# One band-attention and MLP kernel on one core: wider early loads, w_out in column halves, four-bank transpose sessions, and the mask copies moved from slot 1 to slot 10

## The chip, the cores and the metric

The kernel runs on one core of one Trainium2 chip. The metric is device time in microseconds (us) of one execution. A core has these engines: TensorE (PE, with its weight loads shown apart as PEld), VectorE (DVE), ScalarE (ACT), GpSimd (POOL) and SyncE (SP), beside 16 DMA engines that move data. SBUF is the memory on the core that the loads fill, PSUM the one that the matmuls write into, in banks. The granted clock is the share of TensorE's full clock that the profile reports for a stretch of time: 1.00 is full, 0.50 half. The time before the change is 321.6 us (median of three runs, 321.3 to 322.24).

## The reference

The reference takes q, k and v for 8 batches, 8 heads, 576 positions and 64 dimensions. It computes attention within a band of 32 positions to each side, and then a two-layer perceptron with a piecewise activation.

```python
scores = scale * np.matmul(q, k.transpose(0, 1, 3, 2))
mask = np.abs(pos[:, None] - pos[None, :]) <= 32
attn = softmax(np.where(mask, scores, -1e9))          # written out in the reference
x = np.matmul(attn, v).transpose(0, 2, 1, 3).reshape(4608, 512)
h = x @ w_in                                          # 512 -> 2048
g = np.where(h >= 1, h, np.where(h <= -1, 0.0, (h + 1) ** 2 / 4))
out = g @ w_out                                       # 2048 -> 512
```

All inputs and the output are float32. The kernel computes in bfloat16.

## The kernel before

The program is a row of numbered slots. Slot a makes one piece of the hidden layer `hp` (256 tokens by 256 columns, 8 matmuls). ACT and DVE turn it into `gT` (ACT: `rr`; DVE: `mx`, then `gT`). What else has to be done is put between the slots by a table: scores, sums (the attention output `xT`), transposes of q and k (`tp`), and quarters of the second matmul (`op`). Each engine takes its instructions in the order of the program.

First come the parts that the change touches in loading. Every load of q and k for batches 0 to 2 is a piece of 32 partitions (72 KB in SBUF, or 144 KB for the first four, which stay float32), and all but the first four are issued by POOL:

```python
def load_long(b, half, t, y, eng=None, x=None):
    src, dst, nm = ((q, qn, "qn"), (k, kn, "kn"))[t]
    ...
    (eng or nc.gpsimd).dma_start(out=dst[b, half][32 * y:32 * y + 32],
                                 in_=src[b].rearrange("(h y) s d -> y h (s d)", h=2)[y]
                                 .rearrange("h (l p j) -> l p h j", l=2, p=32)[half])

def load_w_out(n):                       # 4 of the 16 row blocks, all 512 columns
    nc.gpsimd.dma_start(out=w_out[:, 4 * n:4 * n + 4], in_=...)

for y in range(NY):                      # NY = 4
    load_long(0, 0, 0, y, nc.sync, q32)
for y in range(NY):
    load_long(0, 0, 1, y)
...
w = [(load_w_in, c, c + 256, h) for c in range(0, DFF, 256) for h in range(2)]
put(w[:4] + halves(0, 1) + w[4:])        # halves: eight loads of 72 KB
mix(halves(1, 0), [(load_w_out, 0)])
put([(load_w_out, 1), (load_w_out, 2)] + [(load_v, 1, n) for n in range(4)])
mix(halves(1, 1), [(load_w_out, 3)])
...
```

Then come the parts of the slots. A transpose session of q or k has two parts (5 and 4 blocks of columns, each for two groups of heads, 18 matmuls together). Each part takes a PSUM buffer of pool `ps_s` or `ps_n`, and each pool has one buffer:

```python
quarters = [(9, 0), (11, 4), (12, 1), (13, 5), (13, 2), (14, 6), (15, 3), (15, 7)]
at(1, *through(0, 1, 0), (keep_warm, 4, ps_o, "op"))    # q of batch 0, second half
at(1.5, *through(0, 1, 1))                              # k of batch 0, second half
at(2, (scores, 0, (0, 1), (0, 2), (2, 4)), (scores8, 0, ps_o))
...
    # in the loop over slots a
    if a == 1:
        for h in range(2):                              # four copies on DVE
            for m, n, w in ((mask4, 8, 128), (mask8, 4, TAIL)):
                V.tensor_copy(m[HD[h]]..., band[HD[h], ...].to_broadcast([64, n, w]))
    run(a)
    for x in post:
        quarter(x)
    run(a + 0.5)
```

The softmax here doesn't subtract the row's maximum and nothing guards it: scores larger than these inputs give would overflow.

## Time and profile before

| | before |
|---|---|
| time, median | 321.6 us |
| profiled execution, span | 319.4 us |
| PE busy | 306.2 us, 96% |
| lines of the profile: hp, op, tp, mx, xT | L463, L414, L178, L469, L296 and L299 |

The prediction shows the page, the stretches and the timeline near 20 us. The view below is the list of waits of PE; the columns are the instruction that waited with its line, what it waited for, then us in total, number of times and the longest.

```profile
PE tp L178 <- DVE qT L181: 2.8, 1, 2.8
PE hp L463 <- DVE xT L299: 1.3, 1, 1.3
...
PE tp L180 <- DVE qb L324: 1.1, 1, 1.1
...
PE hp L463 <- DVE xT L296: 0.8, 2, 0.5
PE bb L284 <- DVE xT L296: 0.6, 1, 0.6
```

It is read from the top. The largest single wait of the bound engine is the second k transpose in slot 1, which waits for the DVE copy of qT. Every other wait is smaller, and none of them is for a DMA.

### The profile page before, as it was taken

How to read it: one execution, taken by the hardware profiler on the slowest of the kernel's cores; microseconds unless marked ns; L12 is line 12 of the kernel's file. 1: busy time of each engine (PE TensorE's matmuls, PEld its weight loads, DVE VectorE, ACT ScalarE, POOL GpSimd, SP SyncE). 2: the span in 40 equal slices, each digit the busy share in tenths (PEclk: the TensorE clock that was granted, in tenths of full speed). 3: DMA queues.
4: the chain of work that ended last, by engine and by line, in shares of the span. 5: the costliest groups of instructions: out<-in, count | busy, mean ns of one | idle time of the engine just before them, and what ended most of it. 6: DMA issues, size and time to landing. Idle time of an engine off the chain costs nothing.

```text
span 319.4 us, 8557 instructions
## 1 busy us (share of the span) xinstructions
PE 306.2 (96%) x3651; PEld 201.8 (63%) x3651; DVE 248.9 (78%) x390; ACT 192.9 (60%) x318; POOL 88.6 (28%) x121
## 2 busy tenths in 40 slices
PE   7969899999999999999999999999999999999995
PEld 3547565666666666666666666666666666666652
DVE  3366956787888888888888888888888888878760
ACT  3739656675785576756766666666676766554421
POOL 8786938896204504130501200000000000000000
PEclk9989999999999999999999999999999999999999
DMA  9999999999999999949990956005410000000111
GB/s 146 161 134 182 168 176 166 170 162 164 152 146 160 168 125 186 161 58 110 187 154 36 109 106 110 35 35 108 95 50 35 33 35 35 36 33 35 49 49 66
DMA packets 122661, 34.52 MB, mean 108 GB/s; under 512 B 108800, under 2 KB 117760, under 8 KB 122624
## 3 DMA queue, kind: packets, MB, share of 16 engines
q0 software_dynamic: 93760, 18.06, 74.4%
q1 hardware_dynamic: 28864, 15.93, 21.9%
q8 instruction: 28, 0.46, 0.6%
q14 instruction: 9, 0.07, 0.1%
HBM read 36.70 MB, written 9.44 MB: 144 GB/s over the span
## 4 chain that ended last, share of the span: by engine, by line
PE 85%; DVE 6%; ACT 5%; DMA 1%; issue 1%; SPq 0%; ACTq 0%; DVEq 0%
PE op L414 38%; PE hp L463 37%; PE bb L284 5%; PE bb L218 2%; DVE mx L469 2%; PE tp L178 2%; ACT pt L226 1%; DVE gT L470 1%; DMA q<-in_q_dram 1%; ACT rc L291 1%; ACT lr L290 1%; ACT rr L467 1%; DVE xT L296 1%; PE bb L197 0%; DVE mask L475 0%
## 5 line engine op out<-in xcount | busy, mean ns | idle before, releaser
L463 PE MATMUL hp<-xT,w_in 128*128 128x256 bf16 x1152 | 150.2, 274 | 2.1 <-DVE xT L299 1.3
L414 PE MATMUL op<-w_out,gT 128*128 128x512 bf16 x576 | 146.6, 380 | 0.0
L467 ACT ACTIVATE rr<-hp 128x512 f32<-128x512 f32 x144 | 85.5, 595 | 92.3 <-PE hp L463 91.1
L463 PEld LDWEIGHTS <-w_in 128*128 128x128 bf16 x1152 | 111.7, 98 | 43.9 <-issue 3.1
L469 DVE TENSOR_TENSOR mx<-hp,rr 128x512 f32<-128x512 f32 x144 | 99.2, 689 | 38.7 <-ACT rr L467 36.8
L470 DVE SCALAR_TENSOR_TENSOR gT<-rr,mx 128x512 bf16<-128x512 f32 x144 | 99.6, 692 | 4.9
L414 PEld LDWEIGHTS <-gT 128*128 128x128 bf16 x576 | 53.4, 98 | 41.6
L226 ACT ACTIVATE pt<-bb 128x1024 bf16<-128x1024 f32 (+1 forms) x33 | 33.2, 1011 | 6.5 <-PE bb L218 5.3
L100 POOL DMA_DIRECT2D vn<-in_v_dram x32 | 27.5, 883 | 28.8 <-PE bb L218 28.2
L296 DVE TENSOR_TENSOR xT<-bb,rc 128x512 bf16<-128x512 f32 (+1 forms) x32 | 21.0, 657 | 10.8 <-ACT rc L291 10.2
L419 ACT COPY osb<-op 128x512 f32<-128x512 f32 x36 | 20.8, 581 | 11.6 <-PE op L414 11.2
L291 ACT ACTIVATE rc<-lr 128x512 f32<-128x512 f32 (+2 forms) x40 | 23.5, 587 | 1.3
L92 POOL DMA_DIRECT2D qn<-in_q_dram x10 | 12.3, 1245 | 41.1 <-DMA qT<-qn 41.1
L290 ACT ACTIVATE lr<-bb 128x512 f32<-128x512 f32 (+2 forms) x40 | 22.0, 551 | 0.7 <-PE bb L284 0.6
L284 PE MATMUL bb<-pt,ones 64*64 64x256 bf16 (+3 forms) x352 | 19.5, 255 | 1.3 <-DVE xT L296 0.6
L192 DVE TENSOR_TENSOR pt<-pt,mask 128x1024 bf16<-128x1024 bf16 (+1 forms) x33 | 20.2, 613 | 0.2 <-ACT pt L226 0.2
L284 PE MATMUL bb<-pt,vn 64*64 64x128 bf16 (+3 forms) x712 | 18.2, 204 | 0.0
L284 PEld LDWEIGHTS <-vn 64*64 64x64 bf16 x712 | 16.7, 107 | 0.0
L284 PEld LDWEIGHTS <-ones 64*64 64x64 bf16 x352 | 10.3, 106 | 9.8 <-issue 9.0
L84 POOL DMA_DIRECT2D kn<-in_k_dram x24 | 13.0, 549 | 9.0 <-DMA w_out<-in_moe_w_out_dram 4.1
L218 PE MATMUL bb<-qT,kT 64*64 64x128 bf16 x520 | 13.0, 217 | 0.8 <-DVE kT L181 0.8
L92 POOL DMA_DIRECT2D kn<-in_k_dram x10 | 12.2, 1226 | 3.6 <-DMA kn<-in_k_dram 2.2
(44 smaller groups left out, 102.7 us busy)
## 6 DMA issues: line engine op xcount, KB each, us to landing
out_dram<-osb SPq DMA_DIRECT2D x36, 256.0 KB, 2.4
vn<-in_v_dram POOLq DMA_DIRECT2D x32, 144.0 KB, 6.0
qn<-in_q_dram POOLq DMA_DIRECT2D x10, 288.0 KB, 6.9
kn<-in_k_dram POOLq DMA_DIRECT2D x10, 288.0 KB, 8.9
w_in<-in_moe_w_in_dram POOLq DMA_DIRECT2D x16, 128.0 KB, 5.5
w_out<-in_moe_w_out_dram POOLq DMA_DIRECT2D x4, 512.0 KB, 7.9
kn<-in_k_dram POOLq DMA_DIRECT2D x24, 72.0 KB, 4.0
qn<-in_q_dram POOLq DMA_DIRECT2D x20, 72.0 KB, 5.5
```

What stands on the lines that cost most here:

```text
L92: nc.gpsimd.dma_start(out=x[:, :, h], in_=src[b, NY * h:NY * h + NY].rearrange("y s d -> (y s) d") .rearrange("(u p) d -> p u d", p=128))
L100: nc.gpsimd.dma_start(out=vn[b][64 * a:64 * a + 64, :, h], in_=v[b, y:y + 2].rearrange("y s d -> (y s) d") .rearrange("(c r) d -> r c d", ...
L226: A.activation(p, ps[:, :, :128 * n].rearrange(like, y=m), AF.Exp, scale=D ** -0.5)
L284: nc.tensor.matmul(bb[HD[h], a, o + c0:o + c1], ones[HD[a]] if c is None else vn[b][HD[a], c, h], p(a, h), start=n == 0, stop=True, skip_g ...
L290: A.activation(lr[:, :, :D0], bb[:, :, D0:2 * D0], AF.Ln)
L291: A.activation(rc[:, :, :D0], lr[:, :, :D0], AF.Exp, scale=-1.0)
L296: muls.append(lambda: V.tensor_mul(o, bb[:, :, :D0], rc[:, :, :D0]))
L414: nc.tensor.matmul(o, gT[tt // 2][:, j, 128 * (tt % 2):128 * (tt % 2) + 128], w_out[:, j], start=not done, stop=len(done) == 2 * NF - 1, s ...
L463: nc.tensor.matmul(hp[:, j], w_in[:, kk, 256 * f + 128 * j:256 * f + 128 * j + 128], xT[:, kk, r0:r0 + TB], start=n == 0, stop=n == 3)
L467: A.activation(rr, hp, AF.Relu, scale=0.5, bias=0.5)
L469: V.tensor_max(mx, hp, rr)
L470: V.scalar_tensor_tensor(gT[t][:, 2 * f:2 * f + 2], rr, 1.0, mx, op0=ALU.min, op1=ALU.mult)
```

## The change

The intent is to start the middle of the program sooner and keep PE from standing near 20 us, in four moves:

- q and k of batches 1 and 2 come in one load each, with rows of nine positions per partition. The first half of batch 0 comes in two loads per tensor, q from SP and ACT, k from POOL; so does its second half, all from POOL (four loads where there were eight). The later columns of w_in come in 512-column pieces.
- w_out is loaded in two halves of 256 columns. A pair of token tiles (256 tokens) uses one half at a time, so that the first output matmuls need half of w_out.
- All 36 transposes of one tensor of a batch (in slot 1, those of the second halves of q and k) run as one session over four PSUM banks. The copies to SBUF come after all of them. Four warming matmuls between them go away.
- The four mask copies on DVE go from slot 1 to slot 10.

The places of later scores, sums and transposes in the table move along with these, as the cuts show.

```diff
-    for y in range(NY):
-        load_long(0, 0, 0, y, nc.sync, q32)
-    for y in range(NY):
-        load_long(0, 0, 1, y)
+    for h in range(2):
+        load_half(0, 0, h, (nc.sync, nc.scalar)[h], q32)
+    for h in range(2):
+        load_half(0, 1, h)
 ...
-    w = [(load_w_in, c, c + 256, h) for c in range(0, DFF, 256) for h in range(2)]
-    put(w[:4] + halves(0, 1) + w[4:])
-    mix(halves(1, 0), [(load_w_out, 0)])
-    put([(load_w_out, 1), (load_w_out, 2)] + [(load_v, 1, n) for n in range(4)])
-    mix(halves(1, 1), [(load_w_out, 3)])
+    w = [(load_w_in, c, c + 256, h) for c in range(0, 1024, 256) for h in range(2)]
+    w += [(load_w_in, c, c + 512, h) for c in range(1024, DFF, 512) for h in range(2)]
+    put(w[:4] + [(load_half, 1, t, h) for t in range(2) for h in range(2)] + w[4:])
+    put([(load_w_out, 0, n) for n in range(2)] + [(load_rows, 1, t) for t in range(2)])
+    put([(load_v, 1, n) for n in range(4)] + [(load_w_out, 1, n) for n in range(2)])
 ...
+    def tposes(b, *sets):
+        todo = []
+        for (t, half), pool in zip(sets, (ps_s, ps_n)):
+            tp = pool.tile([128, 2, 8, 128], BF, name="tp", tag="bb")
+            todo += [tpose(b, 2 * half + part, t, (A.copy, V.tensor_copy)[part], tp[:, part]) for part in range(2)]
+        for copy in todo:
+            copy()
 ...
-    quarters = [(9, 0), (11, 4), (12, 1), (13, 5), (13, 2), (14, 6), (15, 3), (15, 7)]
+    pairs = [(10, 0), (10, 1), (11, 2), (12, 3), (13, 4), (14, 5), (15, 6), (16, 7)]
 ...
-    at(1, *through(0, 1, 0), (keep_warm, 4, ps_o, "op"))
-    at(1.5, *through(0, 1, 1))
+    at(1, (tposes, 0, (0, 1), (1, 1)))
 ...
-    for n, a in enumerate((20, 22, 23, 27)):
+    for n, a in enumerate((18, 20, 22, 27)):
         at(a, seq[2 + n][0])
-    for n, a in enumerate((11.5, 12.5, 19, 20, 22, 26, 27)):
+    for n, a in enumerate((13.5, 14.5, 16, 18, 20, 25, 27)):
         at(a, seq[n][1])
 ...
-    for b, half, *a in ((1, 0, 9.5, 10.5), (1, 1, 17.5, 18.5), (2, 0, 24.5, 25.5), (2, 1, 28.5, 29.5)):
+    for b, *a in ((1, 11.5, 12.5), (2, 19.5, 21.5)):
 ...
-        if a == 1:
+        if a == 10:
             for h in range(2):      # the mask copies
```

Left out are the bodies of `load_half`, `load_rows` and `pair`, and the copy orders that belong to the new layouts.

## The prediction

> **What bounds the kernel now.** I read the page first, then the stretches of 2 us, then the timelines of TensorE (PE), VectorE (DVE) and GpSimd (POOL) where a stretch was not full. The kernel is a row of slots: slot n makes one 256-token, 256-column piece of the hidden layer (hp, 8 matmuls), and quarters of the second matmul (op, 4 matmuls), attention pieces and transposes (tp) are put between. From the page:
>
> ```profile
> PE 306.2 (96%) x3651; PEld 201.8 (63%) x3651; DVE 248.9 (78%) x390; ACT 192.9 (60%) x318; POOL 88.6 (28%) x121
> PE   7969899999999999999999999999999999999995
> DMA  9999999999999999949990956005410000000111
> ```
>
> PE is the bound: 306.2 of 319.4 us busy, and in the stretches after 90 us it has no gap until the last tiles. Only the first 90 us and the way the work is filled in there can give anything: 13.2 us of idle in all, some of it (start, end) untouched. The 16 transfer engines are full for the first 60 us or so, so loads may pace what PE gains. In the 2 us stretches (columns: length, busy time of PE, PEld, DVE, ACT, POOL, granted clock, DMA share, GB/s):
>
> ```profile
> 18.00:20.00 2.00, 1.08 (x14) 0.46 (x12) 1.97 (x5) 1.11 (x2) 2.00 (x4) 1.00 1.19 135
> 20.00:22.00 2.00, 0.15 (x4) 0.15 (x5) 1.75 (x4) 0.00 (x0) 2.00 (x4) 0.84 1.21 143
> 22.00:24.00 2.00, 2.00 (x16) 1.28 (x13) 0.72 (x1) 0.00 (x0) 1.18 (x3) 0.50 1.30 160
> ```
>
> PE stands at 20 to 22 us and then runs at half clock: "busy" at 22 us is not full speed. The timeline says why (start, duration, instruction, idle before it and who ended it); PE and DVE rows together:
>
> ```profile
> 18.61 0.47 PE L178 MATMUL tp<-ident,kn 128*64 128x128 bf16 x10
> 19.54 1.51 DVE L475 COPY mask<-band 64x1024 bf16<-64x1024 bf16 x4
> 21.08 0.72 DVE L181 COPY qT<-tp 128x512 bf16<-128x512 bf16 x1
> 21.85 0.64 PE L178 MATMUL tp<-ident,kn 128*64 128x128 bf16 x8 [2.77 <-DVE qT L181]
> 22.42 1.89 PE L463 MATMUL hp<-xT,w_in 128*128 128x256 bf16 x8
> 24.24 0.64 PE L197 MATMUL bb<-bias,ident 64*64 64x512 bf16 x4
> 33.44 1.91 PE L463 MATMUL hp<-xT,w_in 128*128 128x256 bf16 x16 [1.31 <-DVE xT L299]
> 35.19 1.03 PE L414 MATMUL op<-w_out,gT 128*128 128x512 bf16 x4
> 36.77 1.05 PE L463 MATMUL hp<-xT,w_in 128*128 128x256 bf16 x8
> ```
>
> The second k transpose waits for a PSUM buffer that the DVE copy of qT empties; that copy stands behind the mask copies (1.51 us). Loads at this time:
>
> ```profile
> 14.97 1.05 POOL L84 DMA_DIRECT2D kn<-in_k_dram  x2 [1.31 <-DMA w_in<-in_moe_w_in_dram]
> 16.02 6.21 POOL L104 DMA_DIRECT2D w_in<-in_moe_w_in_dram  x10
> ```
>
> POOL waits for an older load before it issues the next. The program order of its instructions shows it: each load waits on one of eight semaphores in turn, so eight loads are in flight at most, and with 72 KB loads that is little (102 GB/s at 16 to 18 us, against 160 to 200 in most stretches).
>
> **What the Trainium skill says.** (1) "TensorE: Matmul & The Clock Gate", What's actually happening: the clock falls to half after an idle window of about 3.4 us and comes back after a busy one. The trace agrees in kind: clock 0.50 after a 2.77 us wait, the 8 hp matmuls spaced over 1.82 us instead of 0.87. (2) "DMA: Bandwidth & Descriptors", Rules for kernel authors: small transfers should be merged into large ones, and two transfers to disjoint partition groups into one of 128 partitions. The trace shows 0.53 us of POOL for each 72 KB load and the slump above. (3) The same page, Issuing engines are not separate DMA queues: issuing from two engines saves only the issuing time. Here one q issue takes about 0.42 us, and q and k together already move 229 and 196 GB/s at 2 to 6 us, so I expect little from the split over SP and ACT.
>
> **The change, part by part** (shifts of PE's position against before; minus is earlier).
>
> 1. *First loads.* q: two issues on two engines in place of four on one (1.80 us of issuing); k: two on POOL in place of four (2.27 us). The 0.59 MB of q and 0.30 MB of k were all moved by 6 us at over 190 GB/s, so the data, not the issue, sets most of it. The q cast at 6.26 us comes perhaps 0.3 us earlier. **-0.3.**
>
> 2. *Slot 1: one session in four banks, masks gone, four warm matmuls gone.* All 36 transposes now run without a wait (2 x 0.63 us after 17.01). The DVE chain is next: its four hp steps end at 19.54, then qT 0.72 and kT 0.72 give 20.98. In the new program the DVE copy of a session also waits for the ACT copy of it, but ACT is done by about 19.2. So the scores of slot 2 start near 21.0 in place of 24.24. hp of slot 2 (0.87) fits in between if its weights are there: they landed at 20.2, and should land one to two us earlier, because their issue no longer waits behind eight q and k loads. **-3.2**, with the 0.85 us of warm matmuls, the 2.77 us wait and the 0.95 us of half clock all within it. About 1.8 us of idle stays (18.9 to 20.7).
>
> 3. *Slots 2 to 8.* ACT is nearly continuous from exp at 25.16 to 32.5, and DVE from 24.98 to 40; both chains are unchanged, so slot 8 (33.44, waiting for xT on DVE) just moves. Weights for slots 4 and 5 landed at 24.5 and 26.2 and would be needed near 23.5; slot 4 now has to wait for a 512-column piece. I reckon on 0 to 1 us there, partly hidden in ACT's queue. **0.**
>
> 4. *Slots 9 and 10.* Before, a quarter of op (0.87) and 18 transposes (0.63) filled PE at 35.19 to 36.77 while DVE caught up: mx and gT take 0.68 + 0.69 us a slot against 0.87 for hp. Now five hp groups stand in a row, and the fifth needs a PSUM buffer that mx of slot 8 frees (ends 36.64 before). PE stands 1.5 us there; the same work comes later. **+1.5.**
>
> 5. *w_out in column halves.* 64 matmuls of 512 columns become 128 of 256. The last 36 op matmuls take 7.78 us (0.216 each), eight hp matmuls of 256 columns 0.87 (0.109 each), with weight loads of 98 ns beside them: 13.9 us either way. **0.** It lets the first pairs run with half of w_out (1.05 MB) and q and k come sooner.
>
> 6. *Slots 10 to 16.* The masks (1.51) and more DVE copies of transposes fall here, where DVE had 0.9 to 1.2 us idle a slot; I find no wait longer than 0.3 on PE from it. One score set gets its mask from DVE (0.68) in place of PE (-0.25). Up to slot 16 there are 36 more transposes (+1.26) and one quarter less (-0.87). Before slot 16 the chain sums, Ln, exp, xT took 2.8 us (49.4 to 52.19) with two quarters (1.73) under it and 0.52 idle; now only one pair (0.87) lies under it: idle 1.3. **+0.14 + 0.8.**
>
> 7. *Slots 17 to 30.* The second session of each tensor of batch 1 is gone, the work above is paid back (-0.39). Before, PE gaps add up to about 3.8 us between 52 and 88 us (0.57 three times and 0.31, 0.80, 0.25 at attention pieces, and 0.09 at each edge of a transpose). Now two gaps of about 0.9 (sums of slots 20 and 22 waiting for the last DVE copy, itself behind ACT's) and small ones, 2.4 in all. **-0.4 - 1.4.**
>
> After slot 30 nothing changes. Sum: -0.3 - 3.2 + 1.5 + 0.14 + 0.8 - 0.39 - 1.4 = **-2.85 us**, 321.6 to about **318.8 us**.
>
> **Rivals.** (a) *Loads take over*: w_in of slots 4 to 7, or q and k of batch 1, which are now needed whole at slots 11 and 12. At 0.168 MB/us and 4.99 MB moved at 32 us, the 6.4 MB up to k are there near 40.5 us; PE would want them near 40.7. For it: DMA is full. Against it: fewer, larger loads fill the slump. It would leave a gain of 1 us or none (320.5 to 321.5). (b) *All stalls of the first 90 us vanish, nothing replaces them*: 2.8 + 1.3 + 0.8 + 0.6 + 0.5 + 0.4 of waits, 0.85 warm, 1.2 clock: some 8 us, 313. Against it: five hp in a row outrun DVE, and one pair under the slot 15 chain. (c) *The clock falls again*: the 1.8 us left idle near 20 us may still bring half clock; about +1 us (319.8). (d) *DVE becomes the bound* in slots 10 to 16 by masks and copies: another +1.
>
> **Range and chances.** (a), (c), (d) push up by 1 each, (b) in part pulls down by 2: 316.3 to 321.0. Faster by 2% needs under 315.2, which only most of (b) gives: 0.06. Slower by 2% needs a new bound of 6 us: 0.01.
>
> **What would show it.** Right: no PE wait for qT near 20 us, clock 1.0 at 22 us, slot 8 near 30 us; then an hp wait of about 1.5 us for DVE at slot 10, one of over 1 us for xT at slot 16, two of 0.9 at slots 20 and 22; PE busy for op and hp unchanged. Wrong: PE or its weight loads waiting for w_in, qn, kn or w_out; a clock below 1 after 20 us; a start of hp before 14 us or after 15.

## The result and the profile after

| | before | after |
|---|---|---|
| time, median of four runs | 321.46 us (321.3 to 322.24) | 317.26 us (316.82 to 317.79) |
| ratio, with 95% interval | 1 | 0.987 (0.9851 to 0.9888) |
| span of the profiled execution | 319.4 us | 315.0 us |

A ratio here, and below, is the mean time of one kernel's runs over the mean of the other's runs of the same rounds, so it is not quite the ratio of the medians that stand beside it. The kernel is 1.3% faster, which is inside the 2% band called "same". The gain is 4.2 us where 2.85 was predicted.

From the page of the changed kernel (busy us, share of the span and number of instructions; then tenths in 40 slices):

```profile
PE 298.4 (95%) x3670; PEld 207.7 (66%) x3707; DVE 250.8 (80%) x393; ACT 192.1 (61%) x316; POOL 69.5 (22%) x83
PE   8987998999999999999999999999999999999995
DMA  9999999999999969997993983005501100100111
```

The PE row has the same form: full from the eighth slice to the last but one, with all other holes before. The busy time of PE must not be compared with the 306.2 of before: 477 records of `op` from L424 are in this trace where the program has 512, and the holes of the missing ones show as 4.8 us of waits for "issue". The position of an instruction is a safer measure, and I use it from here on. DVE is 1.9 us busier, and POOL went from 121 to 83 instructions.

The 2 us stretches answer to those in the prediction (length, busy time of PE, PEld, DVE, ACT and POOL, granted clock, DMA share, GB/s):

```profile
18.00:20.00 2.00, 1.44 (x12) 0.92 (x12) 1.97 (x5) 1.06 (x2) 2.00 (x3) 1.00 1.27 202
20.00:22.00 2.00, 1.86 (x52) 1.42 (x55) 1.35 (x3) 1.39 (x4) 1.98 (x3) 1.00 1.25 208
22.00:24.00 2.00, 2.00 (x81) 1.66 (x70) 1.36 (x2) 1.97 (x5) 0.85 (x1) 1.00 1.26 194
```

From 20 to 22 us PE is busy for 1.86 us rather than 0.15. From 22 to 24 us the granted clock is 1.00 rather than 0.50, and 81 matmuls, many of them small ones of attention, fit where 16 did. The data rate is about 200 GB/s where it was 135 to 160.

The timeline of PE (start, duration, instruction, idle before it and who ended it):

```profile
16.77 0.90 PE L183 MATMUL tp<-ident,kh 128*64 128x128 bf16 x18
18.19 1.03 PE L484 MATMUL hp<-xT,w_in 128*128 128x256 bf16 x8 [0.52 <-DVE mx L490]
19.53 0.41 PE L202 MATMUL bb<-bias,ident 64*64 64x512 bf16 x4 [0.31 <-DVE qT L186]
20.14 0.42 PE L223 MATMUL bb<-qT,kT 64*64 64x128 bf16 x16 [0.20 <-DVE kT L186]
...
28.90 1.91 PE L484 MATMUL hp<-xT,w_in 128*128 128x256 bf16 x16 [1.05 <-DVE xT L304]
...
32.15 1.03 PE L484 MATMUL hp<-xT,w_in 128*128 128x256 bf16 x8 [1.34 <-DVE mx L490]
33.02 1.91 PE L440 MATMUL op<-w_out,gT 128*128 128x256 bf16 x16
```

And of DVE:

```profile
18.16 0.69 DVE L491 SCALAR_TENSOR_TENSOR gT<-rr,mx 128x512 bf16<-128x512 f32 x1
18.77 0.71 DVE L186 COPY qT<-tp 128x512 bf16<-128x512 bf16 x1
19.38 0.71 DVE L186 COPY kT<-tp 128x512 bf16<-128x512 bf16 x1
...
35.40 1.19 DVE L496 COPY mask<-band 64x1024 bf16<-64x1024 bf16 x4
```

The transposes of k now run without the 2.77 us wait. The hidden piece of slot 2 follows at 18.19 (22.42 before), and slot 8 begins at 28.90 (33.44 before). Slot 10 waits 1.34 us for `mx`, which is the new wait that the prediction had named. The waits of PE, in the same columns as before:

```profile
PE hp L484 <- DVE mx L490: 1.9, 2, 1.3
...
PE hp L484 <- DVE xT L301: 1.1, 3, 0.5
PE hp L484 <- DVE xT L304: 1.1, 1, 1.1
PE bb L289 <- DVE kT L186: 0.8, 1, 0.8
PE bb L289 <- DVE qT L186: 0.8, 1, 0.8
PE bb L289 <- DVE pt L197: 0.4, 1, 0.4
```

With the smaller ones that are not shown, and without those for the first warm-up data and for issue, the listed waits add up to 6.6 us, against 7.8 before. So the waits alone do not make the 4 us: the warming matmuls and the half clock, which count as busy, are in it too, and many of the waits have only changed place. None is for a DMA. The two of 0.8 are the sums of slots 20 and 22, which wait for the last DVE copy of a transpose session.

The issues of POOL (start, duration of the group, instruction, idle before and who ended it):

```profile
11.46 1.93 POOL L109 DMA_DIRECT2D w_in<-in_moe_w_in_dram  x3 [0.16 <-issue]
14.62 2.45 POOL L109 DMA_DIRECT2D w_in<-in_moe_w_in_dram  x4 [1.23 <-DMA w_in<-in_moe_w_in_dram]
```

The weights of slot 2 are issued at 11.5 and 12.1 us and land at 17.4 and 18.1. Before, they were issued at 16.0 and 16.6 us and landed at 19.5 and 20.2.

Where the time went can be read from the starts of the same work in both traces:

| work | before, us | after, us | shift | step's own part |
|---|---|---|---|---|
| slot 0, hp | 14.79 | 14.01 | -0.78 | -0.78 |
| slot 2, scores | 24.67 | 20.14 | -4.53 | -3.75 |
| slot 8, hp | 33.44 | 28.90 | -4.54 | -0.01 |
| slot 16, second part of hp | 52.25 | 50.00 | -2.25 | +2.29 |
| slot 31, hp | 89.64 | 85.65 | -3.99 | -1.74 |
| last hp | 306.65 | 302.67 | -3.98 | +0.01 |
| end of span | 319.4 | 315.0 | -4.4 | -0.4 |

The column at the right is the difference of two neighbouring shifts. Everything is decided by 86 us; between slot 31 and the last hp nothing changes. The last 0.4 us is not work that the change touched: the last output transfer lands at 318.1 us before and at 314.1 after, a shift of -4.0, so the rest lies in the end of the program behind that.

Part of the gain is the clock, and the runs of the kernel before show how much. Of its 33 timed runs in the three sets of experiments, the 24 with a granted clock of 0.995 or lower have a median of 321.66 us, the 9 with 0.997 or higher one of 320.4 us. So about 1.3 us is at stake in whether the clock falls, and the other 3 us of the gain do not need that fall.

### The profile page after: what moved, and what is told of

Same layout as the page of the kernel before. It is cut to its first block, busy times and chain, and to the rows that moved or that the text cites. A ratio compares the mean times of both kernels' runs of the same rounds, so it can differ in the third digit from the quotient of the medians.

```text
span 315.0 us, 8563 instructions
## 1 busy us (share of the span) xinstructions
PE 298.4 (95%) x3670; PEld 207.7 (66%) x3707; DVE 250.8 (80%) x393; ACT 192.1 (61%) x316; POOL 69.5 (22%) x83
## 4 chain that ended last, share of the span: by engine, by line
PE 86%; DVE 5%; ACT 5%; issue 3%; ACTq 0%
PE hp L484 37%; PE op L424 35%; PE bb L289 5%; PE op L440 4%; PE bb L223 2%; PE z L332 2%; DVE mx L490 2%; ACT pt L231 1%; ACT rc L296 1%; DVE gT L491 1%; PE tp L183 1%; DVE xT L301 1%; ACT lr L295 1%; DVE kT L186 1%; DVE qT L186 1%
## 5 line engine op out<-in xcount | busy, mean ns | idle before, releaser
L424 PE MATMUL op<-w_out,gT 128*128 128x512 bf16 x477 | 123.0, 379 | 5.0 <-issue 4.8
L424 PEld LDWEIGHTS <-gT 128*128 128x128 bf16 x512 | 47.6, 98 | 36.7
L301 DVE TENSOR_TENSOR xT<-bb,rc 128x512 bf16<-128x512 f32 (+1 forms) x32 | 21.1, 658 | 11.1 <-ACT rc L296 10.4
L429 ACT COPY osb<-op 128x512 f32<-128x512 f32 x32 | 18.7, 583 | 11.5 <-PE op L424 11.1
L197 DVE TENSOR_TENSOR pt<-pt,mask 128x1024 bf16<-128x1024 bf16 (+1 forms) x34 | 21.0, 616 | 0.2 <-ACT pt L231 0.2
L440 PE MATMUL op<-w_out,gT 128*128 128x256 bf16 x128 | 16.3, 273 | 0.0
L97 POOL DMA_DIRECT2D kn<-in_k_dram x10 | 12.1, 1213 | 9.7 <-PE tp L183 3.9
L440 PEld LDWEIGHTS <-gT 128*128 128x128 bf16 x128 | 12.1, 98 | 1.7
## 6 DMA issues: line engine op xcount, KB each, us to landing
qn<-in_q_dram POOLq DMA_DIRECT2D x2, 576.0 KB, 14.7
```

What stands on the lines that cost most here:

```text
L97: nc.gpsimd.dma_start(out=x[:, :, h], in_=src[b, NY * h:NY * h + NY].rearrange("y s d -> (y s) d") .rearrange("(u p) d -> p u d", p=128))
L424: nc.tensor.matmul(o, gT[tt // 2][:, j, 128 * (tt % 2):128 * (tt % 2) + 128], w_out[:, j], start=not done, stop=len(done) == 2 * NF - 1, s ...
L440: nc.tensor.matmul(o[:, tt], gT[p][:, j, 128 * tt:128 * tt + 128], w_out[:, j, 256 * half:256 * half + 256], start=not done, stop=len(done ...
```

## The experiments

The theory to be tested: about 3.8 us are gained in slot 1, by (i) the mask copies moving away from the qT and kT copies, so that PE neither waits nor loses its clock, together with (ii) merged loads that bring the weights of slots 2 and 3 in time. About 2.3 us are given back in slots 9 to 16, by work placed so that PE waits for DVE. About 1.7 us come back in slots 17 to 30 through fewer copies and waits.

The rivals: the loads alone do it, and the masks do not matter; or the warming matmuls that went are what was gained; or the +2.3 us is contention on DVE and not a matter of placing. Each run was timed in five rounds against the kernel before on the same chip; the medians of the kernel before in the three sets are 321.55, 321.63 and 321.38 us.

| run | median us | ratio to before (95%) |
|---|---|---|
| masks back in slot 1 | 319.61 | 0.9938 (0.9915 to 0.9962) |
| warm matmuls back | 317.43 | 0.9875 (0.9855 to 0.9896) |
| before, masks in slot 10 | 320.0 | 0.9962 (0.9943 to 0.9982) |
| first loads in parts | 318.43 | 0.9915 (0.9893 to 0.9936) |
| second half of batch 0 in parts | 320.26 | 0.9969 (0.994 to 0.9998) |
| pair 0 in slot 9 | 316.83 | 0.9849 (0.9825 to 0.9872) |
| pair 7 in slot 15 | 316.06 | 0.9835 (0.9812 to 0.9858) |
| batch 2's sessions moved | 316.1 | 0.9833 (0.9811 to 0.9855) |
| after, unedited | 317.1 | 0.9875 (0.9843 to 0.9908) |
| w_out in row pieces | 317.99 | 0.99 (0.9873 to 0.9926) |
| three moves together | 315.48 | 0.9815 (0.9791 to 0.9839) |
| the same, one sums piece later | 314.6 | 0.9791 (0.9764 to 0.9818) |

### Masks back in slot 1

```diff
--- after
-        if a == 10:
+        if a == 1:
```

> The changed kernel with the mask copies put back from slot 10 to slot 1, nothing else. Theory (the masks hold up the DVE copies of qT and kT, on which the scores of slot 2 wait): the four copies take 1.2 to 1.5 us, so the scores of slot 2 and all slots up to 8 come 1.2 to 1.5 us later; if PE then idles near 3 us in a row the granted clock falls in the stretch after it and another 0.5 to 1 us is lost. Time 1.2 to 2.2 us over the changed kernel, 318.4 to 319.4. Rival (the four-bank session alone removed the wait, the place of the masks does not matter): no change, 317.0 to 317.5.

The kernel took 319.61 us: about 2.1 us of the change's gain is lost (0.9938 less 0.987 to 0.9875 of some 321 us). That is within the 1.2 to 2.2 us expected, though the median lies 0.2 us above the times named. The PE timeline of this run:

```profile
21.22 0.41 PE L202 MATMUL bb<-bias,ident 64*64 64x512 bf16 x4 [2.10 <-DVE qT L186]
...
22.55 1.89 PE L484 MATMUL hp<-xT,w_in 128*128 128x256 bf16 x8
```

And its stretch from 22 us:

```profile
22.00:24.00 2.00, 2.00 (x35) 1.46 (x28) 1.18 (x2) 1.47 (x3) 0.85 (x1) 0.51 1.27 195
```

With the masks back, the wait for qT is back as 2.10 us even though the transposes are in one session, and the clock is back at half. The eight hp matmuls of slot 3 show 1.89 us, where they show 1.05 at full clock. So the session by itself does not remove the wait; it only moves it from the transposes to the scores. Slot 8 begins at 31.91, 3.0 us later than after. This is one execution with half clock; of the six timed runs one had a clock of 1.000 and still took 319.32 us, so most of the loss needs no fall of the clock. The loads, at 195 GB/s, are as after and cannot be the cause.

### The kernel before with only the masks moved

```diff
--- before
-        if a == 1:
+        if a == 10:
```

> The kernel before with one edit: masks at slot 10 in place of slot 1. Theory: the DVE copy of qT starts at 19.5 in place of 21.1 us, the second k transposes at 20.3, PE's wait falls from 2.8 to about 1.3 us and the clock stays at 1.0 at 22 us; slot 8 starts 2 to 3 us earlier, the time falls by 2 to 3 us to 318.5 to 319.5. Most of the gain of slot 2 is then the masks' alone, and the session adds the last 1 us. Rival (the two-bank session is what holds PE, masks or not): a gain of at most 1.2 us, clock still falling at 22 us.

It took 320.0 us, so 1.2 us (by the ratio) to 1.6 us (by the medians) were gained where 2 to 3 had been expected: a miss. PE's timeline shows both halves of the reason:

```profile
20.33 0.41 PE L178 MATMUL tp<-ident,kn 128*64 128x128 bf16 x8 [1.23 <-DVE qT L181]
...
48.80 1.89 PE L414 MATMUL op<-w_out,gT 128*128 128x512 bf16 x8 [1.99 <-DMA w_out<-in_moe_w_out_dram]
```

The first line is as the theory wants: the wait shrinks from 2.77 to 1.23 us (it remains, I take it, because the sessions here are two-bank ones; that was not run alone), the clock is 1.00 from 20 to 26 us, and slot 8 begins at 30.62, 2.82 us earlier than in the kernel before. The second line is where the gain went: with the loads of the kernel before, PE reaches the output matmuls before the w_out piece is there and waits 1.99 us for it. By the second part of slot 16 (50.74 us) only 1.51 us of the 2.82 are left. Hence rival (a) of the prediction, "loads take over", is real for this kernel. The changed kernel, with its new load order and w_out in halves, shows no such wait.

### The second half of batch 0 in eight loads instead of four

```diff
--- after
+    def load_parts(half, t, eng=None, x=None):      # four loads of 32 partitions, 72 KB each
+        ...
-    put(w[:4] + [(load_half, 1, t, h) for t in range(2) for h in range(2)] + w[4:])
+    put(w[:4] + [(load_parts, 1, t) for t in range(2)] + w[4:])
```

(The copy order of this half changes with its layout.)

> The changed kernel with the second half of batch 0's q and k loaded in eight 72 KB parts again, in place of four loads of 128 partitions. Theory (eight loads in flight at most, so small loads hold up the issue of w_in behind them): w_in of slot 2 is issued near 14 to 15 us in place of 11.5 and lands near 19.5, that of slot 3 near 21.5 to 22.5 in place of 18.7 to 19.4; hp of slot 2 or 3 then waits and slot 8 comes 0.5 to 2 us later, time 317.8 to 319.3. Rival (loads are never on the path here): same landing order with slack, slot 8 at 28.9, time within 0.3 us of the changed kernel.

It took 320.26 us in the median, 319.37 to 322.41, so about 3 us of the gain is lost: the largest effect of any single part taken back, and more than the 0.6 to 2.0 us expected. The profile fell on its slowest execution (322.41), so what it shows is larger than typical. Its waits, from the PE timeline:

```profile
17.93 0.69 PE L191 MATMUL tp<-ident,kh 128*64 128x128 bf16 x18 [0.70 <-DMA kh<-in_k_dram]
20.38 1.03 PE L492 MATMUL hp<-xT,w_in 128*128 128x256 bf16 x8 [1.76 <-DVE kT L194]
...
27.01 1.87 PE L492 MATMUL hp<-xT,w_in 128*128 128x256 bf16 x8 [2.92 <-DMA w_in<-in_moe_w_in_dram]
```

And from POOL's timeline:

```profile
15.34 0.54 POOL L92 DMA_DIRECT2D kh<-in_k_dram  x1 [1.58 <-DMA w_in<-in_moe_w_in_dram]
15.86 4.91 POOL L117 DMA_DIRECT2D w_in<-in_moe_w_in_dram  x8
```

Four more loads, of the same bytes in all, move the first w_in issue after them from 11.46 to 15.86 us, partly because POOL stands 1.58 us until an older load has landed. Slot 2 stands 1.76 us, for the copy of kT by the profile. The w_in piece of slot 4 then comes 2.92 us too late, and in this execution the clock fell during this wait: it was 0.55 from 26 to 28 us, and the eight matmuls at 27.01 show 1.87 us. Two of the six timed runs had a clock of 1.000 and took 319.37 and 319.83 us, so at least 2 us of the loss are there without the fall. The data rate was 90 GB/s from 16 to 18 us, where the changed kernel has 193. Here the masks are in slot 10 and the session is in four banks as after. So moving the masks does not pay in this kernel unless the loads come in time. The two are not all or nothing, however. With all of the change but the masks, slot 8 comes 1.53 us earlier than before; with the masks alone, 2.82 us. Together these are 4.35, near the 4.54 of the changed kernel (one profile each).

### First loads in parts, as before

```diff
--- after
-    for h in range(2):
-        load_half(0, 0, h, (nc.sync, nc.scalar)[h], q32)
-    for h in range(2):
-        load_half(0, 1, h)
+    load_parts(0, 0, nc.sync, q32)
+    load_parts(0, 1)
```

> The changed kernel with the first q and k loads as before: four q loads on SP, four k loads on GpSimd. Theory (the fewer, wider first loads brought the first hp 0.78 us forward): the first hp at 14.7 to 14.8 in place of 14.0 us, the time 0.6 to 0.9 us more, 317.9 to 318.2. Rival (my prediction: the data and not the issue sets it): 0.3 us or less. If the start moves and the end does not, later loads or DVE absorb it.

It took 318.43 us, about 1.2 us more than after, where 0.6 to 0.9 was expected. The start itself moved little: the first hp came at 14.31 us (14.01 after, 14.7 to 14.8 expected). But the w_in of slot 2 is issued at 12.99 rather than 11.46 us, and PE waits for data that it does not wait for after. From its list of waits:

```profile
PE hp L490 <- DMA w_in<-in_moe_w_in_dram: 1.2, 2, 0.7
...
PE tp L189 <- DMA kh<-in_k_dram: 0.6, 1, 0.6
```

Slot 4 begins at 23.88, 1.27 us later than after, of which 0.30 was there at the first hp; slot 8 begins at 30.33, 1.43 us later. (Between them lies a wait of 0.93 us just before slot 5 that the profile puts down to "issue". It is 0.20 us in the first profile of the changed kernel and 1.20 in the repeat below, so I do not count it as an effect of this edit.) The first loads are therefore worth more downstream, through POOL's place in its queue, than at the start.

Why the start moves so little shows when the ACT cast of q and PE's first rows are put side by side. Before:

```profile
6.26 0.62 ACT L325 CAST qb<-q 128x512 bf16<-128x512 f32 x1 [4.24 <-DMA q<-in_q_dram]
6.94 0.68 PE L180 MATMUL tp<-ident,qb 128*128 128x128 bf16 x9 [1.05 <-DVE qb L324]
```

After:

```profile
1.19 5.15 PE L332 MATMUL z<-warm 128*128 128x512 bf16 x14 [1.19 <-DVE warm L126]
4.98 0.62 ACT L339 CAST qb<-q 128x512 bf16<-128x512 f32 x1 [2.29 <-DMA q<-in_q_dram]
6.18 0.67 PE L185 MATMUL tp<-ident,qb 128*128 128x128 bf16 x9
```

The cast comes 1.28 us earlier. The transposes come only 0.76 us earlier, and they wait for nothing now: the 14 warming matmuls, which end at about 6.2 us, are what holds PE. When they end differs from execution to execution, because the clock rises at different times. In the changed kernel's profile they start 0.43 us apart at first and 0.22 us apart from 5.3 us on. In the profile of the run with pair 0 in slot 9 (the same start) they last 5.83 us and the transposes begin at 6.87. In the profiles of kernels with this start the first hp is at 13.92 to 14.88 us. The two profiles with the first loads of before and nothing else changed in the start, the kernel before and the run with only its masks moved, have 14.79 and 14.82. The start is thus worth between 0 and 0.9 us in one execution.

### Warm matmuls back

```diff
--- after
-        for (t, half), pool in zip(sets, (ps_s, ps_n)):
+        for n, ((t, half), pool) in enumerate(zip(sets, (ps_s, ps_n))):
+            if b == 0 and n == 1:
+                keep_warm(4, ps_o, "op")
```

> The changed kernel with the four warm matmuls put back between the q and the k transposes of slot 1. Theory (PE now waits for DVE in slots 1 and 2 anyway, 0.52 us before hp of slot 2 and 0.5 us before the scores): the 0.85 us of warm matmuls are hidden but for a rest, the scores of slot 2 stay at 20.1 us, time within 0.3 us of the changed kernel, 317.0 to 317.6. Rival (they were 0.85 us of PE time on the path, and leaving them out was part of the gain): 0.8 to 0.9 us more, near 318.1.

It took 317.43 us, which cannot be told from the changed kernel (317.26, and 317.1 in another set). The scores of slot 2 begin at 20.07 us (20.14 after). The 0.85 us of warming matmuls lie in time in which PE would stand anyhow, since DVE's copies set the start of the scores. So the rival that their removal is the gain falls.

### Pair 0 in slot 9, pair 7 in slot 15

These two test whether the +2.29 us of slots 8 to 16 is a matter of placing.

```diff
--- after, one run each
-    pairs = [(10, 0), (10, 1), (11, 2), (12, 3), (13, 4), (14, 5), (15, 6), (16, 7)]
+    pairs = [(9, 0), (10, 1), (11, 2), (12, 3), (13, 4), (14, 5), (15, 6), (16, 7)]
+    pairs = [(10, 0), (10, 1), (11, 2), (12, 3), (13, 4), (14, 5), (15, 6), (15, 7)]
```

> The changed kernel with the first op pair moved from slot 10 to slot 9. Theory (the 1.34 us in which hp of slot 10 waits for DVE's mx is PE time without work, since five hp groups stand in a row): the pair's 0.87 us fills it, its w_out half landed at 27.5 us, everything from slot 10 on comes 0.8 to 0.9 us earlier, time 316.3 to 316.5. Rival (DVE is the bound of slots 8 to 16, so filling PE only moves the wait): the wait of slot 10 shrinks but waits of slots 11 to 16 grow, time within 0.3 us of the changed kernel.

> The changed kernel with op pair 7 moved from slot 16 to slot 15, under the chain sums, Ln, exp, xT that hp of slot 16 waits for. Theory: the two waits for xT (0.33 and 0.51 us) go, time 0.7 to 0.85 us less, 316.4 to 316.6. Rival (pair 7 needs gT of slots 14 and 15, which DVE makes at 45.6 to 48.5 us, so PE waits for gT instead): the wait moves to op, gain 0.2 us or less.

With pair 0 in slot 9, the wait of slot 10 becomes 0.47 us (1.34 after). From the PE timeline:

```profile
32.83 1.03 PE L484 MATMUL hp<-xT,w_in 128*128 128x256 bf16 x8 [0.47 <-DVE mx L490]
```

From slot 8 to the second part of slot 16 it takes 20.47 us where the changed kernel takes 21.10: 0.63 us less, not the 0.87 of one pair. By its position the k session near 39.5 us now loses the other 0.24 us; the profile lists no wait there, so what it waits for (DVE's copies of the q session, I take it) is not shown. The whole kernel took 316.83 us. With one profile for each, and the start differing by up to 0.9 us, the stretch says more than the total.

With pair 7 in slot 15, slot 8 to slot 17 takes 23.07 us instead of 23.95, 0.88 less: the waits for `xT` at L301 go from 1.1 us in three pieces to 0.2 in one. The whole took 316.06 us, about 1 us less, and 0.3 us under the 316.4 to 316.6 expected. Both waits are thus a matter of which work lies under a chain of ACT and DVE: 0.63 + 0.88 = 1.51 of the +2.29 us came away by placing alone.

### Sessions of batch 2 earlier

```diff
--- after
-    for n, a in enumerate((18, 20, 22, 27)):
+    for n, a in enumerate((18, 21, 22, 27)):
         at(a, seq[2 + n][0])
-    for b, *a in ((1, 11.5, 12.5), (2, 19.5, 21.5)):
+    for b, *a in ((1, 11.5, 12.5), (2, 16.5, 19.5)):
```

> The changed kernel with the two transpose sessions of batch 2 moved from after slots 19 and 21 to after slots 16 and 19, and one sums from slot 20 to 21, so that no sums follows a session in the next slot. Theory (the sums of slots 20 and 22 wait 0.77 us each for the last DVE copy of the session before them): both waits go, time 1.2 to 1.6 us less, 315.7 to 316.1. Rival (the same DVE work must be done somewhere and some other matmul waits for it, or q of batch 2 lands too late for slot 16): gain under 0.5 us.

It took 316.1 us. From the second part of slot 16 to slot 24 it takes 20.55 us instead of 21.41, 0.86 less, where 1.2 to 1.6 was expected. Both waits of 0.77 us are gone from the list, but some of it comes back in another. From the PE waits:

```profile
PE bb L289 <- DVE xT L301: 0.3, 1, 0.3
```

The rest must lie in gaps too short for the list; where, is not shown. The median is at the edge of the 315.7 to 316.1 expected; in the trace the size was missed and the direction held.

### The changed kernel again, and w_out in row pieces

```diff
--- after (the unedited kernel is the other run)
-    pairs = [(10, 0), (10, 1), (11, 2), (12, 3), (13, 4), (14, 5), (15, 6), (16, 7)]
+    pairs = [(10, 0), (10, 4), (11, 1), (12, 5), (13, 2), (14, 6), (15, 3), (16, 7)]
-            (pair if x < 4 * 4 else quarter)(x)
+            quarter(x)
     # and load_w_out loads 4 of the 16 row blocks with all 512 columns
```

> The changed kernel again, unedited, as the measure of the others of this call and to see how far its early times move between executions. Expected: ratio to before 0.985 to 0.989; in the profile the first hp between 13.9 and 14.7 us (seen so far in kernels with the same start), slot 8 at 28.8 to 29.6, waits for w_in of 0 to 1.2 us in slots 2 to 4. If slot 8 moves by 0.7 us with the first hp, then the 0.78 us of the start is partly spread, not the first loads alone.

> The changed kernel with w_out in four row pieces and 512-column quarters again, in the slots that the pairs have, two row pieces where each column half stood in the order of loads. Theory (the column halves let all work of slots 10 to 16 run on the first 1.05 MB of w_out; by rows, slot 13 needs the third piece, which lands near 42.6 us and slot 15 the last, near 46.4): PE waits about 1 us for w_out at slot 13 and perhaps again at slot 15, time 0.5 to 1.5 us over the changed kernel. Rival (a matter of form only: 64 matmuls of 512 columns for 128 of 256, 13.9 us either way): within 0.3 us.

The unedited kernel took 317.1 us, with a ratio of 0.9875, as in its first measurement. In its profile slot 8 begins at 29.42, where the first profile has 28.90. Slot 2 waits 0.76 us for w_in here, but that is made up at once: slot 3 begins at 20.73 (20.66 in the first profile). The delay comes just before slot 5, in a wait of 1.20 us (0.20 in the first profile) that the profile puts down to "issue"; its cause is not known. This is the size of what one profile can differ from another of the same program. One of its six runs had a clock of 0.995 and took 319.04 us.

With w_out in row pieces it took 317.99 us, 0.9 us more than the unedited kernel in the same set. PE's waits in this run:

```profile
PE op L424 <- DMA w_out<-in_moe_w_out_dram: 0.9, 1, 0.9
```

The quarter in slot 13 waits for the third piece of w_out. The column halves are worth about that much, by the data's arrival and not by the matmuls' own time.

### All three moves together

```diff
--- after
-    pairs = [(10, 0), (10, 1), (11, 2), (12, 3), (13, 4), (14, 5), (15, 6), (16, 7)]
+    pairs = [(9, 0), (10, 1), (11, 2), (12, 3), (13, 4), (14, 5), (15, 6), (15, 7)]
-    for n, a in enumerate((18, 20, 22, 27)):
+    for n, a in enumerate((18, 21, 22, 27)):      # second run: (18, 21, 23, 27)
         at(a, seq[2 + n][0])
-    for b, *a in ((1, 11.5, 12.5), (2, 19.5, 21.5)):
+    for b, *a in ((1, 11.5, 12.5), (2, 16.5, 19.5)):
```

> The three schedule edits together: pair 0 to slot 9, pair 7 to slot 15, the sessions of batch 2 after slots 16 and 19 with one sums at slot 21. Alone they gave 0.6, 0.9 and 0.9 us in the traces. If each fills a wait of its own they add up: 2.2 to 2.6 us less than the changed kernel, about 314.8, ratio 0.978 to 0.981. If they share one bound (DVE in slots 8 to 22), less: 1.5 us or under.

> As the run with all three edits, and the sums of slot 22 moved to 23, since in the run with the sessions moved the sums of slot 22 waited 0.3 us for xT of those of slot 21. Expected: 0.2 to 0.5 us less than with slot 22. If the wait goes to another matmul: no difference.

They took 315.48 and 314.6 us. The second is the fastest version: 2.1% less than the kernel before (0.9791, 0.9764 to 0.9818), and 2.5 us less than the unedited changed kernel in the same set. As both intervals contain 0.98, whether either is faster by the 2% rule is unclear.

Neither expectation held by the medians. The first run gained 1.6 us and not 2.2 to 2.6; the second gained another 0.9 and not 0.2 to 0.5, with three of its six runs near 314.1 and three from 315.0 to 315.3. The traces are closer to what was expected: from slot 8 to slot 31 it takes 56.75 us in the changed kernel, 54.80 in the first run and 54.42 in the second. So the first gains 1.95 there, against 0.63 + 0.88 + 0.86 = 2.37 for the moves alone, and the later sums piece another 0.38. From the second run's list of waits of PE:

```profile
PE hp L484 <- DVE xT L304: 1.3, 1, 1.3
...
PE bb L202 <- DVE qT L186: 1.1, 1, 1.1
PE hp L484 <- DVE mx L490: 0.5, 1, 0.5
PE bb L289 <- DVE pt L197: 0.4, 1, 0.4
```

The wait of slot 8 (1.3) and those of slots 1 and 2 stay; of the four waits that the moves aimed at, the one for `mx` is down to 0.5, and the others are gone or at 0.2. In this profiled execution the start was late (first hp at 14.88), so it is not even the start that makes it faster.

## Why the prediction was right or wrong

The class, the range (316.3 to 321.0) and most of the mechanism held; the time was 1.5 us below the figure, more than half of the gain forecast. That the class and the range held despite it owes something to their width. Step by step:

1. **First loads: -0.3 predicted, -0.78 in the two profiles.** The reason given, that the bytes and not the issue set the time, is wrong in part: the cast of q came 1.28 us earlier and not 0.3. What limited the gain was something that the step did not look at, the warming matmuls ahead of the transposes. By execution the gain is 0 to 0.9 us. The step also left out that fewer loads on POOL bring the w_in of slot 2 forward. In the profile of the run with first loads in parts slot 4 is 1.27 us late, and 0.97 of that comes after the start, where PE waits for k and w_in. The sentence on issuing engines that the prediction cites was too readily taken as "little". But that run undoes the width of the loads and the split over SP and ACT together; the split alone was not run, and stays open.

2. **Slot 1: -3.2 predicted, -3.75 measured.** The mechanism is shown: with the masks back, a wait of 2.10 us and half clock are back. In the profile of the kernel before with the masks alone moved, the scores begin at 21.90 us, 2.77 earlier; the other 1.0 us belongs to the rest of the change (the session, the loads, the warm matmuls), and only for the warm matmuls does a run show that it is not theirs. The prediction's absolute time for the scores was close. It said near 21.0 us before any shift of the start, and 20.14 + 0.78 = 20.92 was measured. What was mis-sized is the other end of the subtraction. The scores were set against 24.24 us, the start of the mask matmuls of before, but the scores themselves began at 24.67. That is 0.43 of the 0.55 us. The rest is near 0.1, and it lies in DVE's copies: they start 0.61 us apart although each is listed with 0.71 us, so two of them end sooner than twice 0.72. The 1.8 us of idle time that the step left standing was too much as well: the listed waits are 0.52, 0.31 and 0.20, or 1.0 us. The demand that the weights come in time was named in the step, and the run with the second half in parts shows that it is a condition: without it nearly all of the gain is gone (ratio 0.9969).

3. **Slots 2 to 8: 0 predicted, -0.01 measured** (-4.53 at the scores of slot 2, -4.54 at slot 8). In the first profile no piece of w_in was late. In the repeat slot 8 was 0.52 us later, but not by a late piece of w_in. The wait for w_in in slot 4 that the step allowed for, 0 to 1 us, is there in one profile with these loads, that of the run with the warm matmuls back: 0.56 us.

4. **Slots 9 and 10: +1.5 predicted; a wait of 1.34 measured**, for `mx` as named. Putting one pair into slot 9 takes 0.87 of it away, though only 0.63 us stays gained by slot 16.

5. **w_out in halves: 0 predicted for the matmuls.** This can't be read from the busy times, as records are missing. But the run with full-width quarters shows no gain for them: it is 0.9 us slower, and 0.87 us of that is one wait for w_out.

6. **Slots 10 to 16: +0.94 predicted.** Steps 4 and 6 can only be compared as a sum, since the work put off in slot 9 comes back there: +2.44 predicted, +2.29 measured from slot 8 to slot 16. The waits at slots 15 and 16 are 0.39 + 0.33 + 0.51 = 1.23 us; the step had 1.3. It was one of three pieces rather than one, and the first of them is for the masked `pt`, not for `xT`.

7. **Slots 17 to 30: -1.79 predicted, -1.74 measured.** Between these two points are 36 transposes less and one quarter more, -0.39 us as predicted, which leaves -1.35 for the gaps (-1.4 predicted). The waits that the profile lists there hardly differ (1.8 us before, 1.5 after), so most of that gain lies, by subtraction, in gaps too short for the list; no run tested it by itself. The two waits are 0.77 us each where about 0.9 was said, at the slots that were named and for the reason that was named.

The measured parts give -0.78 - 3.75 - 0.01 + 2.29 - 1.74 = -3.99 us, against -2.85. So nearly the whole miss is in steps 1 and 2 (-1.03 of -1.14), where one cost was read from the wrong row and one earlier transfer was under-rated.

Of the rivals, (a) did not come true in the changed kernel; it did in the kernel before with only the masks moved (1.99 us for w_out) and in the run with the second half in parts (2.92 us for w_in). Rival (b) came true only in so far as the -3.75 was larger. Placing some pieces of work anew then gave 2.5 us more, so a good part of what (b) hoped for could be had by placing. Rival (c) did not happen in the profiled execution, where the clock was 1.00 throughout. It is a matter of executions all the same: one of the ten timed runs of the unedited kernel had 0.995. Of the 33 timed runs of the kernel before in the three sets, 24 were at 0.995 or lower. Rival (d) was not seen: PE's waits for DVE in slots 10 to 16 are those listed, and the mask copies at 35.40 us end none of them. Of its kind is only the 0.39 us for the masked `pt`, which the kernel before does not have.

What stays open: how much of step 1 is the split over SP and ACT; whether fewer warming matmuls would let the transposes start with the cast; what the four-bank session alone is worth, since no run takes it back by itself; what the wait before slot 5 is; and how the runs that took back one part each add up. Taken back alone, the masks cost 2.1 us, the merged loads of the second half 3, the first loads 1.2 and the w_out halves 0.9. This is more than the whole gain, so the parts do not add up. For the two smaller ones the interval overlaps with that of the repeated kernel.

## What to carry to other kernels

A wait on one engine is worth removing only if the next thing it would wait for, here the weights and then w_out, comes earlier too: check the transfers at the new times before counting on the gain, because the same edit of the masks was worth 2.1 us in the changed kernel and 1.2 in the kernel before, both by their ratios, and there a wait of 1.99 us for w_out took part of it back. When a DVE copy stands between two TensorE stages, put one-off work such as filling masks anywhere but ahead of it. Measure a shift between two starts of the same instruction group, and look at what else holds the engine (here warming matmuls) before saying what an earlier transfer is worth.

## What the Trainium skill lacked or had wrong

- "TensorE: Matmul & The Clock Gate", Why this matters for your kernels, advises no TensorE gaps of more than about 3 us. In these runs a shorter one was enough: half clock came with a wait of 2.10 us (0.51 in the stretch after it) and with one of 2.77 us (0.50). Waits of 1.34 us, and one of 1.99 us, left it at 1.00, in the executions profiled. Around the wait of 2.77 us PE was sparsely busy (1.08 of 2 us and 0.15 of 2 us in the two stretches of the kernel before). The page tells of short idles that bring the clock down, in A second HAM failure mode, but gives no share of busy time below which that happens.
- The same page, What's actually happening, calls the window free-running and the cold count different from run to run. These runs agree: the same 14 warming matmuls took 5.15 us in one execution and 5.83 us in another, and the kernel before was granted 0.989 to 1.000 over 33 executions. What the page lacks is that this can move everything behind it, here by 0.96 us at the first hp (13.92 to 14.88 us in the profiles with this start).
- "DMA: Bandwidth & Descriptors", Rules for kernel authors, advises merging small transfers, and the runs agree. It lacks what a small one costs a program whose loads queue behind one another: eight 72 KB loads in place of four of 144 KB cost about 3 us; the trace shows 0.54 us of POOL for a load and a wait of 1.58 us for an older load to land.
